# State times queries by four heads at a time: quadrants of the array, two output banks, permuted rows of the first weight matrix

## The chip, the core and the metric

The kernel runs on one core of one Trainium2 chip. The metric is the device time of one execution in microseconds; three executions of the kernel before took 618.56, 619.71 and 620.05 us, median 619.71 us.

## The reference

Three layers follow each other. The first is attention with decay ("retention"): 2 batches, 8 heads, 768 tokens, 64 features a head, in float32. In blocks of tokens

```python
intra = np.einsum('bhic,bhjc->bhij', qb, kb) * Dmask[None]
intra = np.einsum('bhij,bhjd->bhid', intra, vb)
inter = np.einsum('bhid,bhde->bhie', qb * lam_pow[None], kv_state)
out[:, :, sl] = intra + inter
...
kv_state = lam_block[None, :, None, None] * kv_state + np.einsum('bhsd,bhse->bhde', kb_dec, vb)
```

The result, 1536 tokens by 512 features (8 heads of 64), goes through two feed-forward layers: `g(x @ w_in) @ w_out` with `w_in` 512 by 2048 and g a clipped square, then `((x @ w_a) * (x @ w_b)) @ w_out` with inner width 1536. Those weights are float64 in memory.

## The kernel before

**Attention.** It takes blocks of 128 tokens: 12 chunks c, six to a batch. For each chunk `load_chunk` (L143) brings four tiles of 256 KB: q and k by feature (for head h = 2 pr + e, its 64 features stand in partitions 64e to 64e + 63 and its 128 tokens in columns 128 pr), k and v by token. Then, per chunk:

- `att_scores` (L150): eight products of keys and queries, even heads into one PSUM bank, odd heads into another. `att_mask` (L180, VectorE) multiplies both banks with the decay mask into two SBUF tiles.
- `att_kd` (L161) and `att_qd` (L172), on GpSimd: keys and queries times powers of the decay.
- `att_state` (L194, then L205 or L208 and L209): the new state of each head, 64 by 64, kept in `st` with even heads in the lower 64 partitions and odd heads in the upper 64.
- `att_out`: for every chunk but the first of a batch eight products "state times q" (L221), each with 64 rows and 64 columns of TensorE's array; even heads use rows and columns 0 to 63, odd heads rows and columns 64 to 127. Then eight products "weights times v" (L225), with 128 rows and 64 columns, even and odd heads in turn, are added in the same bank. One ScalarE copy (L237) rounds the bank to the type of the matmuls (the "high" part), and one VectorE subtraction (L241) gives the remainder (the "low" part); both stand in `block`, from where `xy` takes them as four groups of 128 features.

Each of these fp32 matmuls is executed as two passes, so the trace has 16 MATMUL records for eight products. PSUM banks come from seven that are handed out in turn (`bank`, L61).

**Feed-forward.** `mm3` (L358) makes each product of three matmuls, high times high, high times low, low times high. `h_bank` is one 128 by 512 tile of the first layer's inner matrix: 12 matmuls, then L376 (VectorE), L377 (ScalarE), L379 (VectorE) and the split of the result by L265 (ScalarE) and L266 (GpSimd). The weights arrive as float64 by `load_w` (L261, issued by SyncE) and are made into high and low tiles by `weight_pieces` (L280 and L281 on ScalarE, L294, L298, L302 and L311 on VectorE, then L265 and L266); `bg(n)` places n such pieces between other work.

**Order.** The order on every engine is written out by hand: chunks 0 to 3 first, then a loop over nb and j in which `h_bank(j, nb)` stands ahead of the output of chunk 4 + 4 nb + j; all of attention is over by 96 us. From then on the feed-forward layers run to the end. SyncE issues the loads in program order; a DMA also waits until the one issued eight places earlier in the program has landed, since all DMAs share eight completion counters in turn.

Of the kernel before, what the change touches and what calls it, by code (L numbers as in the profile page):

```python
# [9 lines left out]
F32 = mybir.dt.float32  # L10
F32R = mybir.dt.float32r
BF16 = mybir.dt.bfloat16
I32 = mybir.dt.int32
U32 = mybir.dt.uint32
ACTF = mybir.ActivationFunctionType
ALU = mybir.AluOpType

B, H, S, D = 2, 8, 768, 64
CH = 128
# [4 lines left out]
KT = DM // 128  # L24
# [11 lines left out]
def retention_ffn_kernel(ctx: ExitStack, tc: tile.TileContext, lam, att, w1i, w1o, w2ab, w2o, out):  # L36
# [7 lines left out]
    nc = tc.nc  # L44
# [9 lines left out]
    block = [const.tile([128, KT, 2, 512], F32R, name=f"block{i}") for i in range(NB)]  # L54
# [6 lines left out]
    def bank():  # L61
        banks.rotate(-1)
        return banks[-1]
# [6 lines left out]
    def free2(*tiles):  # L70
        two.extend(tiles)
# [61 lines left out]
    ck = {}  # L133
    sc = {}
    pm = {}
    kd = {}
    qd = {}
# [73 lines left out]
    def att_out(c):  # L211

        cc = c % CPB
        o = bank()
        s = st[cc % 3]
        pairs = [(pr, slice(pr * 128, (pr + 1) * 128)) for pr in range(H // 2)]
        if cc:
            for pr, cols in pairs:
                for e in range(2):
                    r = slice(64 * e, 64 * e + 64)  # L220
                    nc.tensor.matmul(out=o[r, cols], lhsT=s[r, pr, :], rhs=qd[c][r, cols], start=(pr == 0), stop=False)  # L221
        for pr, cols in pairs:
            for e in range(2):
                h = 2 * pr + e
                nc.tensor.matmul(  # L225
                    out=o[64 * e:64 * e + 64, cols],
                    lhsT=ck[c][3][:, h * D:(h + 1) * D],
                    rhs=pm[c][e][:, pr * CH:(pr + 1) * CH],
                    start=(cc == 0 and pr == 0),
                    stop=(pr == H // 2 - 1),  # L230
                )
        nb, t0 = c // 4, (c % 4) * CH
        if nb not in xy:
            xy[nb] = [block[nb][:, k] for k in range(KT)]
        o4 = o.rearrange("p (a i) -> p a i", a=KT)
        hi, lo = (block[nb][:, :, i, t0:t0 + CH] for i in range(2))
        nc.scalar.copy(hi, o4)  # L237
        free2(*pm.pop(c))
        if cc:
            free2(qd.pop(c))  # L240
        return lambda: nc.vector.tensor_tensor(out=lo, in0=o4, in1=hi.bitcast(F32), op=ALU.subtract)  # L241

    def att_done(c):
        loads.append(ck.pop(c)[3])
# [10 lines left out]
    srcs = {"1i": w1i, "1o": w1o, "2i": w2ab, "2o": w2o}  # L255

    def load_w():
        if todo_loads:
            key = todo_loads.popleft()
            r = raw_p.tile([128, 1024], I32, tag="raw", name="raw")  # L260
            nc.sync.dma_start(out=r, in_=srcs[key[0]][key[1]].bitcast(I32))  # L261
            raws[key] = r

    def split_act(src, hi, lo, engine=None):
# [19 lines left out]
    def weight_pieces():  # L284

        nxt = None
        for n, key in enumerate(order):
# [15 lines left out]
                out=v, in0=high, scalar=-0x40000000, in1=word, op0=ALU.bitwise_and, op1=ALU.bitwise_or  # L303
            )
            load_w()
            if 4 <= n + 1 < len(order):
                if order[n + 1] not in raws:
                    load_w()
                nxt = begin(order[n + 1])
# [210 lines left out]
    powers()  # L520
    load_chunk(0, (0, 1))
    load_w()
    load_chunk(0, (2, 3))
    load_chunk(1, (0, 1))
# [17 lines left out]
    bg(2)  # L542
    att_mask(0)
    low0 = att_out(0)
    att_qd(0, nc.gpsimd)
    att_kd(1, nc.gpsimd)
# [4 lines left out]
    add1 = att_state(1)  # L551
    add1()
    low1 = att_out(1)
    att_done(1)
    att_scores(2)
# [4 lines left out]
    add2 = att_state(2)  # L560
    add2()
    low2 = att_out(2)
    att_done(2)
    bg(1)
# [22 lines left out]
    for nb in range(2):  # L587
        for j in range(4):
            c = 4 + 4 * nb + j
            low = []  # L590
# [6 lines left out]
            low = att_out(c)  # L597
# [33 lines left out]
    for i in range(2, len(stages)):  # L631
        g, nb = stages[i]
# [76 lines left out]
```

## Time and profile before

| | us |
|---|---|
| median of three executions | 619.71 (618.56 to 620.05) |
| the profiled execution | 620.09 |
| span of the profiled execution, first to last instruction | 618.3 |
| TensorE matmuls busy | 597.7 (97% of the span) |
| VectorE busy | 457.3 (74%) |
| GpSimd busy | 278.5 (45%) |
| ScalarE busy | 267.8 (43%) |

PE is TensorE's matmul side and PEld its weight loads; DVE is VectorE, ACT is ScalarE, POOL is GpSimd, SP is SyncE. Times in the trace count from the span's start. Matmuls overlap in the array, so a record's duration is longer than its share of the engine: two records that follow each other closely may start nearly together. An arrow "<-" behind an idle time names what ended it.

### The profile page before, as it was taken

To read this page: it belongs to the slowest core of one execution; us is meant where nothing else is said; L and a number is where in the kernel's file an instruction comes from. 1 tells how busy PE (TensorE), PEld (TensorE's weight loads), DVE (VectorE), ACT (ScalarE), POOL (GpSimd) and SP (SyncE) were. 2 spreads that over 40 slices of the span, in tenths; PEclk is the share of its full clock that TensorE was granted. 3 is DMA by queue.
4 is the path that set the end of the run, shared out by engine and by line. 5 is a ranking of instruction groups with operands and counts; after the bars stand their busy time and mean duration, and the time that the engine had idled before them with its cause. 6 is when DMAs were issued, how large, how long until landed. Compare 5 with 4: busy or idle time off the path is not lost.

```text
span 618.3 us, 8380 instructions
## 1 busy us (share of the span) xinstructions
PE 597.7 (97%) x3100; PEld 488.4 (79%) x3100; DVE 457.3 (74%) x684; ACT 267.8 (43%) x473; POOL 278.5 (45%) x218
## 2 busy tenths in 40 slices
PE   7797899999999999999999999999999999999997
PEld 3676678888888888888888788888888888888886
DVE  1578861964975786497869997989979979979553
ACT  1245552655642553264545456434424424424110
POOL 3535570443522543352947655553453553543420
PEclk9799899999999999999999999999999999999999
DMA  5965520221310212131101222302302202300004
GB/s 176 378 247 203 184 92 1 75 96 68 103 64 10 98 68 69 34 103 49 55 1 35 68 87 83 103 34 90 95 21 96 92 18 93 100 14 1 0 23 182
DMA packets 20937, 52.72 MB, mean 85 GB/s; under 512 B 2584, under 2 KB 4896, under 8 KB 20896
## 3 DMA queue, kind: packets, MB, share of 16 engines
q1 hardware_dynamic: 19624, 51.52, 24.3%
q10 hardware_dynamic: 1272, 0.67, 0.4%
q8 instruction: 24, 0.39, 0.3%
q14 instruction: 17, 0.14, 0.1%
HBM read 49.03 MB, written 3.15 MB: 84 GB/s over the span
## 4 chain that ended last, share of the span: by engine, by line
PE 82%; DVE 8%; ACT 4%; POOL 2%; issue 2%; DMA 1%; ACTq 0%; DVEq 0%; POOLq 0%
PE ps L358 79%; DVE words L294 1%; PE ps L225 1%; PE ps L221 1%; DVE two L302 1%; DVE words L298 1%; DVE two L401 1%; DMA lamp<-in_lam 1%; ACT words L280 1%; DVE two L311 1%; PE ps L150 1%; DVE two L180 1%; DMA rows<-base 1%; ACT four L265 1%; ACT two L281 0%
## 5 line engine op out<-in xcount | busy, mean ns | idle before, releaser
L266 POOL TENSOR_TENSOR four<-two,four 128x512 fp32r<-128x512 f32 x109 | 143.1, 1319 | 213.6 <-ACT four L265 203.4
L358 PE MATMUL ps<-block,four 128*128 128x512 f32 x828 | 196.9, 391 | 1.4 <-POOL block L266 1.4
L358 PEld LDWEIGHTS ps<-block,four 128*128 128x128 f32 x828 | 154.6, 188 | 35.4 <-POOL block L266 1.8
L358 PE MATMUL ps<-four,four 128*128 128x512 f32 x633 | 162.0, 389 | 0.0
L358 PEld LDWEIGHTS ps<-four,four 128*128 128x128 f32 x633 | 118.7, 188 | 24.9 <-issue 0.2
L265 ACT CAST four<-two 128x512 fp32r<-128x512 f32 x109 | 67.1, 620 | 93.4 <-DVE two L451 23.7
L266 POOL TENSOR_TENSOR late_four<-two,late_four 128x512 fp32r<-128x512 f32 x47 | 62.2, 1329 | 56.8 <-ACT late_four L265 49.5
L358 PE MATMUL ps<-block,late_four 128*128 128x512 f32 x324 | 77.2, 389 | 0.0
L358 PEld LDWEIGHTS ps<-block,late_four 128*128 128x128 f32 x324 | 60.8, 188 | 12.6
L280 ACT ACTIVATE words<-raw 128x512 f32<-128x512 f32 x68 | 43.1, 634 | 55.0 <-DVE two L302 49.7
L358 PE MATMUL ps<-four,late_four 128*128 128x512 f32 x243 | 64.0, 389 | 0.0
L377 ACT ACTIVATE two<-two,half 128x512 f32<-128x512 f32 x42 | 30.2, 720 | 70.4 <-DVE two L376 70.4
L294 DVE TENSOR_SCALAR words<-words 128x512 f32<-128x512 f32 x68 | 47.0, 691 | 17.4 <-ACT words L280 17.4
L358 PE MATMUL ps<-late_four,four 128*128 128x512 f32 x213 | 58.5, 389 | 0.0
L358 PEld LDWEIGHTS ps<-four,late_four 128*128 128x128 f32 x243 | 45.6, 188 | 9.5
L464 DVE TENSOR_TENSOR two<-two,ps 128x512 f32<-128x512 f32 x62 | 42.2, 680 | 13.1 <-PE ps L358 13.1
L311 DVE CUSTOM_DVE_ANT_0 two<-two,two 128x1024 uint16<-128x1024 uint16 x54 | 49.7, 921 | 1.9
L376 DVE TENSOR_SCALAR two<-ps 128x512 f32<-128x512 f32 x42 | 28.7, 684 | 29.9 <-PE ps L358 29.4
L298 DVE TENSOR_SCALAR words<-words 128x512 int32<-128x512 int32 x68 | 47.5, 699 | 2.3
L426 DVE TENSOR_TENSOR two<-two,ps 128x512 f32<-128x512 f32 x50 | 32.9, 682 | 19.2 <-PE ps L358 16.7
L358 PEld LDWEIGHTS ps<-late_four,four 128*128 128x128 f32 x213 | 40.0, 188 | 8.3
L265 ACT CAST late_four<-two 128x512 fp32r<-128x512 f32 x47 | 28.9, 620 | 36.4 <-DVE two L440 11.4
(99 smaller groups left out, 596.3 us busy)
## 6 DMA issues: line engine op xcount, KB each, us to landing
load<-in_att SPq DMA_DIRECT2D x48, 256.0 KB, 5.3
raw<-in_w2ab SPq DMA_DIRECT2D x24, 512.0 KB, 3.2
raw<-in_w1i SPq DMA_DIRECT2D x16, 512.0 KB, 3.4
raw<-in_w1o SPq DMA_DIRECT2D x16, 512.0 KB, 3.3
raw<-in_w2o SPq DMA_DIRECT2D x12, 512.0 KB, 3.2
out<-two SPq DMA_DIRECT2D x7, 256.0 KB, 2.0
dmask<-rows SPq DMA_DIRECT2D x2, 256.0 KB, 4.6
out<-late_two SPq DMA_DIRECT2D x2, 256.0 KB, 2.0
```

The source lines that it names most:

```text
L150: nc.tensor.matmul(out=sc[c][h % 2][:, pr * CH:(pr + 1) * CH], lhsT=kT[p0:p0 + 64, pr * CH:(pr + 1) * CH], rhs=qT[p0:p0 + 64, pr * CH:(pr ...
L265: nc.scalar.copy(hi, src)
L266: (engine or nc.gpsimd).tensor_tensor(out=lo, in0=src, in1=hi.bitcast(F32), op=ALU.subtract)
L280: nc.scalar.activation(out=words, in_=r[:, :, 1].bitcast(F32), func=ACTF.Abs)
L294: nc.vector.tensor_scalar(out=words, in0=words, scalar1=HIGH_MIN, scalar2=HIGH_MAX, op0=ALU.max, op1=ALU.min)
L298: nc.vector.tensor_scalar(out=word, in0=word, scalar1=3, scalar2=0x3FFFFFFF, op0=ALU.logical_shift_left, op1=ALU.bitwise_and)
L311: nc.vector.tensor_tensor(out=v, in0=v, in1=c, op=ALU.add)
L358: nc.tensor.matmul(out=ps, lhsT=l[a], rhs=r[b], start=(start and i == 0 and j == 0), stop=(stop and i == n - 1 and j == 2))
L376: nc.vector.tensor_scalar(out=r, in0=ps, scalar1=-1.0, scalar2=1.0, op0=ALU.max, op1=ALU.min)
L377: nc.scalar.activation(out=r, in_=r, func=ACTF.Square, scale=0.5, bias=half)
L426: add = lambda o, x, ps: nc.vector.tensor_tensor(out=o, in0=x, in1=ps, op=ALU.add)
L464: nc.vector.tensor_tensor(out=total, in0=total, in1=ps, op=ALU.add)
```

## The change

`att_out` takes two banks in place of one, one for even heads and one for odd heads. "State times q" goes in two groups of four heads; within a group the four products lie in the four quadrants of the array: even heads in the lower 64 rows and odd heads in the upper 64, as the state lies, and now one even and one odd head in each half of the columns. The eight products of weights and v come even heads first, then odd heads, alternating between the halves of the columns. Each bank is filled in 256 columns, and has its own copy and its own subtraction. The features so come out in another order, and `load_w` brings the rows of the first weight matrix ("1i", 16 tiles) in that order, with four DMAs of 128 KB in place of one of 512 KB, in runs of 1 KB in place of 4 KB.

```diff
     def att_out(c):
-        o = bank()
+        o = [bank(), bank()]
...
         if cc:
-            for pr, cols in pairs:
-                for e in range(2):
-                    r = slice(64 * e, 64 * e + 64)
-                    nc.tensor.matmul(out=o[r, cols], lhsT=s[r, pr, :], rhs=qd[c][r, cols], start=(pr == 0), stop=False)
+            for b in range(2):
+                for e, side in ((0, 0), (1, 1), (0, 1), (1, 0)):
+                    p, w = 64 * e, 2 * b + side
+                    nc.tensor.matmul(
+                        out=o[e][64 * side:64 * side + 64, b * CH:(b + 1) * CH], lhsT=s[p:p + 64, w, :],
+                        rhs=qd[c][p:p + 64, w * CH:(w + 1) * CH], start=(b == 0), stop=False,
+                    )
...
+        for e in range(2):
+            for w in range(H // 2):
+                b, side = w // 2, w % 2
+                h = 2 * w + e
+                nc.tensor.matmul(
+                    out=o[e][64 * side:64 * side + 64, b * CH:(b + 1) * CH],
+                    lhsT=ck[c][3][:, h * D:(h + 1) * D],
+                    rhs=pm[c][e][:, w * CH:(w + 1) * CH],
+                    start=(cc == 0 and b == 0),
+                    stop=(b == 1),
+                )
+            o2 = o[e][:, 0:2 * CH].rearrange("p (a i) -> p a i", a=2)
+            hi, lo = (block[nb][:, 2 * e:2 * e + 2, i, t0:t0 + CH] for i in range(2))
+            nc.scalar.copy(hi, o2)
+            parts.append((lo, o2, hi))
...
+        def low():
+            for lo, o2, hi in parts:
+                nc.vector.tensor_tensor(out=lo, in0=o2, in1=hi.bitcast(F32), op=ALU.subtract)
...
     def load_w():
...
+            if key[0] == "1i":
+                for i in range(4):
+                    side, e = i // 2, i % 2
+                    nc.sync.dma_start(
+                        out=r[64 * side:64 * side + 64, 512 * e:512 * e + 512].rearrange("p (b f) -> p b f", b=2),
+                        in_=src[64 * e:64 * e + 64].rearrange("p (b c f) -> p b c f", b=2, c=2)[:, :, side],
+                    )
```

On TensorE, the output of chunk 1 before (L221 state times q, L225 weights times v; `ps` are banks, `st` the state, `two` the decayed queries or the masked weights, `load` is v):

```order
L221 MATMUL ps_114<-two_99,st_148 64x128 x8
L225 MATMUL ps_114<-two_100,load_126 64x128
L225 MATMUL ps_114<-two_101,load_126 64x128
L225 MATMUL ps_114<-two_100,load_126 64x128
L225 MATMUL ps_114<-two_101,load_126 64x128
...
L150 MATMUL ps_115<-load_127,load_128 128x128
```

and in the changed kernel (L222 and L234 are the new lines of the two products):

```order
L222 MATMUL ps_115<-two_99,st_148 64x128
L222 MATMUL ps_116<-two_99,st_148 64x128
L222 MATMUL ps_115<-two_99,st_148 64x128
L222 MATMUL ps_116<-two_99,st_148 64x128
...
L234 MATMUL ps_115<-two_100,load_126 64x128 x4
L234 MATMUL ps_116<-two_101,load_126 64x128 x4
L150 MATMUL ps_117<-load_127,load_128 128x128
```

The two masked weight tiles, two_100 of the even heads and two_101 of the odd heads, alternated; now the four products that read two_100 stand ahead of the four that read two_101, and the two halves go to two banks. The banks that follow move on by one.

On ScalarE, the copies of chunks 1 and 2 before, then in the changed kernel (L243 is the new line of the copy):

```order
L237 CAST block_71<-ps_114 128x4x128
L208 ACTIVATE st_147<-st_149,tabq 128x64 x4
L237 CAST block_71<-ps_111 128x4x128
L280 ACTIVATE words<-raw 128x512
```

```order
L243 CAST block_71<-ps_115 128x2x128
L243 CAST block_71<-ps_116 128x2x128
L208 ACTIVATE st_147<-st_149,tabq 128x64 x4
L243 CAST block_71<-ps_113 128x2x128
L243 CAST block_71<-ps_114 128x2x128
L302 ACTIVATE words<-raw 128x512
```

One copy of 512 columns became two of 256, in the same place; VectorE's subtractions are split in the same way. L280 and L302 are the same instruction of `weight_pieces` (in the changed file 22 lines lower).

On SyncE, the loads of weight tiles 1i-1 to 1i-3 with chunk 3 between them (load_131 to load_134) and the first of chunk 4 (load_121), before, with the counter that each waits for:

```order
L261 DMA raw<-in_w1i 128x1024 [waits DMAHW5_49]
L143 DMA load_131<-in_att 128x512 [waits DMAHW6_49]
...
L143 DMA load_134<-in_att 128x512 [waits DMAHW1_49]
L261 DMA raw<-in_w1i 128x1024 [waits DMAHW2_49]
L261 DMA raw<-in_w1i 128x1024 [waits DMAHW3_49]
L261 DMA raw<-in_w1o 128x1024 [waits DMAHW4_49,DVE_49,Activation_49]
L143 DMA load_121<-in_att 128x512 [waits DMAHW5_49,Pool_49]
```

and in the changed kernel:

```order
L278 DMA raw<-in_w1i 64x2x256 [waits DMAHW0_49]
...
L143 DMA load_134<-in_att 128x512 [waits DMAHW7_49]
L278 DMA raw<-in_w1i 64x2x256 [waits DMAHW0_49]
L278 DMA raw<-in_w1i 64x2x256 [waits DMAHW1_49]
...
L278 DMA raw<-in_w1i 64x2x256 [waits DMAHW7_49]
L283 DMA raw<-in_w1o 128x1024 [waits DMAHW0_49,DVE_49,Activation_49]
L143 DMA load_121<-in_att 128x512 [waits DMAHW1_49,Pool_49]
```

The quarters of 1i-2 and 1i-3 alone now take all eight counters, and load_121, two places behind them, waits for a quarter of 1i-2 to land.

## Rows read from the trace of the kernel before

**Rows 1.** The page's first part: busy time, share of the span, instructions.

```profile
PE 597.7 (97%) x3100; PEld 488.4 (79%) x3100; DVE 457.3 (74%) x684; ACT 267.8 (43%) x473; POOL 278.5 (45%) x218
```

**Rows 2.** Busy time by stretch, eight stretches from 95 to 618 us: their sum.

```profile
sum 523.00, PE 518.22 PEld 427.94 DVE 399.35 ACT 227.33 POOL 232.26; mean PE 64.78 PEld 53.49 DVE 49.92 ACT 28.42 POOL 29.03
```

**Rows 3.** Chain that ended last, in order of time, 0 to 170 us: start, us, what.

```profile
21.85 1.97 PE ps L221 x16
...
27.96 1.02 PE ps L221 x16
...
30.08 0.59 ACT block L237
...
34.50 1.09 PE ps L225 x14
...
61.31 0.67 DVE block L241
...
68.36 0.57 ACT block L237
...
79.63 1.68 POOL two L172
...
95.51 74.58 PE ps L358 x328
```

**Rows 4.** Timeline of TensorE, three short stretches: start, us, line, count, [idle before].

```profile
18.21 0.32 PE L225 MATMUL ps<-two,load 128*64 128x128 f32 x1 [2.50 <-DVE two L180]
...
87.90 0.33 PE L221 MATMUL ps<-two,st 64*64 64x128 f32 x2
...
88.71 0.28 PE L221 MATMUL ps<-two,st 64*64 64x128 f32 x2
88.92 0.33 PE L225 MATMUL ps<-two,load 128*64 128x128 f32 x2
```

**Rows 5.** Groups by line: names, shapes, count, busy us, mean ns, idle before.

```profile
L241 DVE TENSOR_TENSOR block<-ps,block 128x512 fp32r<-128x512 f32 x12 | 8.3, 690 | 9.4 <-ACT block L237 9.4
...
L237 ACT CAST block<-ps 128x512 fp32r<-128x512 f32 x12 | 7.0, 582 | 12.5 <-PE ps L225 12.5
...
L209 DVE TENSOR_TENSOR st<-st,ps 128x256 f32<-128x256 f32 x8 | 3.3, 418 | 2.0 <-ACT st L208 1.3 <-PE ps L194 0.6
...
L205 ACT COPY st<-ps 128x256 f32<-128x256 f32 x2 | 0.7, 362 | 0.0
```

**Rows 6.** Timeline 56 to 97 us: state times q of chunks 7 and 9.

```profile
64.77 1.97 PE L221 MATMUL ps<-two,st 64*64 64x128 f32 x16 [4.62 <-POOL two L172]
...
81.35 1.09 PE L221 MATMUL ps<-two,st 64*64 64x128 f32 x16 [0.90 <-POOL two L172]
```

**Rows 7.** Busy time by stretch; behind POOL's count stands the granted clock.

```profile
16.57:19.98 3.41, 1.52 (x16) 1.04 (x16) 3.24 (x6) 0.67 (x2) 1.70 (x2) 1.00 1.05 370
19.98:23.39 3.41, 2.67 (x30) 2.48 (x32) 1.11 (x2) 1.50 (x5) 3.41 (x4) 0.50 1.04 391
23.39:26.80 3.41, 3.41 (x31) 2.75 (x30) 0.41 (x1) 1.03 (x4) 2.38 (x3) 0.50 1.05 401
...
64.35:67.76 3.41, 2.99 (x26) 2.66 (x28) 3.38 (x5) 2.27 (x4) 1.64 (x2) 0.50 0.73 219
```

**Rows 8.** Timeline 36 to 60 us: the subtraction of chunk 5 (with the wait before it).

```profile
53.93 0.69 DVE L241 TENSOR_TENSOR block<-ps,block 128x512 fp32r<-128x512 f32 x1 [0.21 <-ACT block L237]
```

**Rows 9.** Line L261, SyncE's issue of the w1i tiles: ns min/median/max, first and last.

```profile
L261 SPq DMA_DIRECT2D raw<-in_w1i x16: 327/328/433, 2.5 to 221.5; - x16
```

**Rows 10.** DMA queues from 18 to 33 us.

```profile
DMA packets 2658, 5.91 MB, mean 394 GB/s; under 512 B 297, under 2 KB 297, under 8 KB 2656
```

**Rows 11.** The page's DMA issues: count, KB each, median us from issue to landing.

```profile
raw<-in_w1i SPq DMA_DIRECT2D x16, 512.0 KB, 3.4
...
dmask<-rows SPq DMA_DIRECT2D x2, 256.0 KB, 4.6
```

**Rows 12.** Timeline 27 to 36 us: chunk 4's decayed keys, chunk 4's scores.

```profile
32.52 1.04 POOL L161 TENSOR_TENSOR two<-load,kdf 128x512 f32<-128x512 f32 x1 [5.21 <-DMA load<-in_att]
...
35.52 0.64 PEld L150 LDWEIGHTS ps<-load,load 64*128 64x128 f32 x10 [0.17 <-issue]
```

More of the change, by code (lines that the diff above doesn't have):

```diff
@@ L213, in att_out @@
         cc = c % CPB
-        o = bank()
+        o = [bank(), bank()]
         s = st[cc % 3]
-        pairs = [(pr, slice(pr * 128, (pr + 1) * 128)) for pr in range(H // 2)]
         if cc:
-            for pr, cols in pairs:
-                for e in range(2):
-                    r = slice(64 * e, 64 * e + 64)
-                    nc.tensor.matmul(out=o[r, cols], lhsT=s[r, pr, :], rhs=qd[c][r, cols], start=(pr == 0), stop=False)
[L222 to L231, printed above, removed]
+            for b in range(2):
[5 more added lines that the diff above has]
+                    )
         nb, t0 = c // 4, (c % 4) * CH
@@ L234, in att_out @@
             xy[nb] = [block[nb][:, k] for k in range(KT)]
-        o4 = o.rearrange("p (a i) -> p a i", a=KT)
-        hi, lo = (block[nb][:, :, i, t0:t0 + CH] for i in range(2))
-        nc.scalar.copy(hi, o4)
+        parts = []
+        for e in range(2):
[13 more added lines that the diff above has]
+            parts.append((lo, o2, hi))
         free2(*pm.pop(c))
@@ L240, in att_out @@
             free2(qd.pop(c))
-        return lambda: nc.vector.tensor_tensor(out=lo, in0=o4, in1=hi.bitcast(F32), op=ALU.subtract)
+        def low():
+            for lo, o2, hi in parts:
+                nc.vector.tensor_tensor(out=lo, in0=o2, in1=hi.bitcast(F32), op=ALU.subtract)
+        return low
     def att_done(c):
@@ L260, in load_w @@
             r = raw_p.tile([128, 1024], I32, tag="raw", name="raw")
-            nc.sync.dma_start(out=r, in_=srcs[key[0]][key[1]].bitcast(I32))
+            src = srcs[key[0]][key[1]].bitcast(I32)
+            if key[0] == "1i":
[5 more added lines that the diff above has]
+                    )
+            else:
+                nc.sync.dma_start(out=r, in_=src)
             raws[key] = r
```

## The prediction

> **What bounds the kernel.** I read the busy times first: TensorE's matmuls fill 97% of the span [rows 1]. Then the stretches: from 95 us to the end TensorE is busy 518.22 of 523.00 us [rows 2], and in the chain of waits one unbroken run of L358 begins at 95.51 [rows 3]. So the feed-forward part is TensorE's, the change doesn't touch its instructions, and what the change can move is when TensorE gets to 95.5 us. Before that the chain changes hands. From 21.85 to 30.08 it is TensorE, with the outputs of chunks 1 and 2. Then it goes to ScalarE's copy at 30.08 and, by way of the masks, to the weights product of chunk 3 at 34.50. From there to 79.63 it is mostly VectorE and ScalarE, and at the end GpSimd with the decayed queries of chunk 9 (L172). From 81.35 it is TensorE again, with the outputs of chunks 9, 10 and 11 [rows 3, 6]. Faster products of state and q count only in the first and the last of these pieces, five of ten chunks; in the middle the same change makes VectorE and ScalarE slower.
>
> **Four quadrants.** The 16 passes of L221 take 1.02 us at the full clock [rows 3]. The timeline shows how: the first two records start together at 87.90, the last two together at 88.71, and the next line follows at 88.92 [rows 4]. So eight pairs follow each other, some 0.11 us apart (0.81 us over seven steps, 0.116). A pair is one even and one odd head, not the two passes of one head: where the odd head still waits for its mask, at 18.21, one record starts alone [rows 4], although that head's second pass is next in the program. The array therefore starts a later head in a free quadrant past the waiting second pass of an earlier one. With four free quadrants I expect four to start together and four rounds in place of eight: 4 x 0.11 = 0.44 us less, 0.58 in place of 1.02. No row shows four at once, so the bounds are 0 and 0.44; I take 0.44, since the pairs already pass over one waiting matmul and each quadrant has only two passes in a group.
> The Trainium skill says otherwise ("TensorE: Matmul & The Clock Gate", section "The mechanism"): matmuls begin and end strictly in program order. By that rule a head's second pass holds up all that follow, no more than two quadrants ever overlap, and the saving would be 0. The record that starts alone, against the two that start together, speaks against it as far as one waiting pass goes [rows 4].
>
> **The sum, along the chain** (lead = how much earlier than before).
> - Chunk 1, at 21.85: the product takes 1.97 us, at a granted clock of 0.50, which is 1.2 GHz and lasts from 19.98 to 26.80 [rows 3, 7]. It saves 0.9. But the clock rises about when it did before, and scores that ran at 2.4 GHz slide into the slow stretch, so half of it is left: 0.45. Chunk 2 at 27.96: 0.44; its masks wait for scores that are earlier too. Say 0.85 together at the end of chunk 2's output.
> - The copy: 582 ns for 512 columns [rows 5]. For 256 the nearest row is the state's copy, 362 ns [rows 5]. The first half's copy runs beside the odd heads' products, so after the last product ScalarE needs 0.36 in place of 0.58: lead 0.85 + 0.22 = 1.07 at 30.08.
> - The subtraction: 690 ns; a half costs what L209 does, 418 [rows 5]. Two make 0.84, 0.15 more. VectorE is behind the copy there, so the masks of chunk 3 keep 0.92.
> - Chunk 3's weights: before, 14 of 16 passes wait for the second mask, because even and odd heads alternate, and take 1.02 us from 34.50 [rows 3] to the scores at 35.52 [rows 12]. Now the eight even passes run during the second mask and eight are left: three rounds fewer, 0.33. Lead 1.25 as the first `h_bank` begins.
> - The middle. Two copies cost 0.72 in place of 0.58: 0.14 each where ScalarE ends last, for chunks 4 and 7 (68.36) [rows 3]. Two subtractions cost 0.15 where VectorE does, chunk 6 (61.31) [rows 3]. For chunk 5 VectorE waits 0.21 for the copy [rows 8]; the first half comes 0.22 sooner, and it evens out. Together 0.43: lead 0.82 as the decayed queries of chunk 9 are ready.
> - Chunks 9, 10, 11 on TensorE: 3 x 0.44 = 1.32.
> Sum: 2.1 us.
>
> **What I cost at nothing.** The banks: chunks of the loop now take six of the seven in an iteration and took five, so scores wait for the product or mask of the iteration before. VectorE has done those before TensorE comes there; by the order of the program the closest is chunk 5's, where the state's addition still ends later. If VectorE fell further behind, scores would wait first. The loads: 16 tiles with three issues more each of 0.33 us [rows 9]; SyncE waits for counters and buffers most of the time. Runs of 1 KB: the mask's table, in runs of 512 B, lands in 4.6 us for 256 KB [rows 11], no worse than the others in that stretch. From 18 to 33 us the queues move 394 GB/s [rows 10] whatever the issue, as long as enough is in flight; that is the third rival.
>
> 620.09 - 2.1 = 618.0 for the profiled execution, which is 0.38 above the median of the three; so 617.6.
>
> **Rivals.**
> - *No more than two quadrants at a time.* Then 0.22 - 0.15 + 0.33 - 0.43: nothing is left, 619.7, the same. For it: no row shows four. Against it: rows 4. The rule of the Trainium skill quoted above would give this time. 0.2.
> - *TensorE, now faster, loses its clock.* Ahead of chunk 9 it waits 0.90 us for GpSimd [rows 6]. The outputs of chunks 7 and 8 lie in front; they become 0.9 (chunk 7 starts at 64.77, at the low clock) and 0.44 shorter, GpSimd is only 0.82 earlier, so the wait grows to 1.3 to 1.9 us. A stretch with little work, 16.57 to 19.98, was followed by one at half the clock that lasted 6.8 us; another lasted 3.4 us [rows 7]. From 81 us on TensorE is the path, so 3.4 us at 1.2 GHz cost 1.7 and 6.8 cost 3.4: 619.3, or with the longer one 620.9, slower than before. The longer one decides the sign. 0.15 in all, a third of it the longer.
> - *The loads come late.* Eight counters filled by quarters hold 1 MB: at 394 GB/s 2.6 us of work. A whole tile lands 3.4 us after its issue [rows 11], 1.3 of it transfer, so a quarter needs about 2.4. That is barely enough; two such rounds (1i-2 and 1i-3, then what waits for them) could cost up to 5 us at worst. Chunk 4's keys land at 32.52, its scores start at 35.52 [rows 12] and would start at 34.3; so from 1.8 us of delay it eats the lead, and 5 us would give 3.2 - 2.1 = 1.1 slower, 620.7. 0.07.
> - Something I didn't price: 0.03.
>
> **How the numbers follow.** A measurement of this kernel can tell about 0.3% (1.9 us) from no change. The forecast, 0.55, is 617.6; its own range is 616.8 (masks or copies overlap better) to 618.6 (a product saves 0.3). It lies just beyond 617.85, so I give it 0.34 of "faster", the rest of it to "same". Unpriced gains add 0.05: faster 0.39. Slower by over 0.3%, above 621.6, needs the long low clock or late loads and more: 0.08. Same 0.53. Range 616.7 to 620.4: it takes in the first rival and most of the second.
>
> **What would show it.** Right: L222 with 16 records in about 0.58 us from its start to the next line, four starting together; L243 near 360 ns and L251 near 420; the first `h_bank` product about 1.2 us earlier, the state products of chunk 9 about 0.8, the long run of L358 about 2.1. Wrong: L222 still near 1.02; a granted clock of 0.50 after 81 us; a wait for DMA ahead of chunk 4's scores; scores waiting for VectorE because of a bank.

## The result and the profile after

The changed kernel takes **622.37 us** (median of 9 runs, 621.56 to 624.51) against 619.47 (617.88 to 621.14, 9 runs) for the kernel before: ratio 1.0051, 95% interval 1.0035 to 1.0068. It is slower by 0.35 to 0.68%, where 617.6 was forecast. The profiled execution took 624.23 us, span 622.4. It is one of the longest of its nine, 1.9 over the median, which matters below where the clock is costed.

The page of the changed kernel, its first part, its DMA total and its chain by engine:

```profile
PE 596.2 (96%) x3100; PEld 487.2 (78%) x3100; DVE 458.0 (74%) x696; ACT 268.5 (43%) x485; POOL 278.3 (45%) x218
...
DMA packets 27849, 52.72 MB, mean 85 GB/s; under 512 B 3352, under 2 KB 13856, under 8 KB 27808
...
PE 80%; DVE 7%; DMA 5%; ACT 3%; SPq 2%; issue 2%; POOL 1%; ACTq 0%; DVEq 0%; POOLq 0%
```

DMA and SyncE's queue now hold 7% of the chain, some 44 us; before, DMA had 1% and SyncE none. To see where the end moved, follow TensorE's timeline (start, us, line, count, idle time before and its releaser). The first stretch is where attention hands over to the feed-forward part, the second chunk 9, the last the long run to the end:

```profile
33.09 1.26 PE L234 MATMUL ps<-two,load 128*64 128x128 f32 x16 [1.43 <-DVE two L180]
37.61 2.08 PE L150 MATMUL ps<-load,load 64*128 64x128 f32 x16 [3.27 <-DMA load<-in_att]
39.62 5.04 PE L380 MATMUL ps<-block,four 128*128 128x512 f32 x12
44.59 1.16 PE L150 MATMUL ps<-load,load 64*128 64x128 f32 x16
...
86.44 0.67 PE L222 MATMUL ps<-two,st 64*64 64x128 f32 x16 [1.04 <-POOL two L172]
...
99.21 11.18 PE L380 MATMUL ps<-four,four 128*128 128x512 f32 x48
```

The scores of chunk 5 (44.59 above) and the long run, in the same view of the kernel before:

```profile
39.71 1.16 PE L150 MATMUL ps<-load,load 64*128 64x128 f32 x16
...
95.44 11.18 PE L358 MATMUL ps<-four,four 128*128 128x512 f32 x48
```

Read it in three steps. Chunk 4's scores (37.61) wait 3.27 us for queries and keys; before, they began at 35.52 with no such wait [rows 12]. The scores and the first `h_bank` products then take 2.08 and 5.04 us, where at the full clock they take 1.16 and 3.0, so that chunk 5's scores come 4.9 us later than before. And the products of state and q of chunk 9 begin at 86.44 (before 81.35 [rows 6]), the long run at 99.21 (before 95.44). So nearly the whole loss is made by 44 us and the tail gives 1.3 of it back. From the long run to the end little changed: 622.4 - 99.2 = 523.2 us, 618.3 - 95.4 = 522.9 before.

The clock, by stretches of that timeline (busy time of the engines, granted clock, DMA share, GB/s):

```profile
33.00:37.16 4.16, 1.26 (x16) 0.83 (x16) 2.82 (x7) 1.36 (x3) 0.00 (x0) 1.00 0.83 282
37.16:43.99 6.83, 6.38 (x26) 5.28 (x27) 1.29 (x2) 0.00 (x0) 3.52 (x3) 0.50 1.00 378
```

TensorE works 1.26 of 4.16 us, and the stretch behind it runs at 0.50 (1.2 GHz), 6.83 us of it. Before, the low stretches of [rows 7] end at 26.80 and begin again at 64.35, with 1.00 between.

Why the keys are late stands in SyncE's queue (issues, in order of time):

```profile
22.83 7.24 SPq L278 DMA_DIRECT2D raw<-in_w1i  x8
30.17 0.52 SPq L283 DMA_DIRECT2D raw<-in_w1o  x1
30.80 5.97 SPq L143 DMA_DIRECT2D load<-in_att  x8
```

The quarters of two tiles hold the queue for 7.24 us, so the loads of chunks 4 and 5 are issued from 30.80 (before from 23.02). And the queues move less while that lasts; 18 to 33 us of the changed kernel, against 394 GB/s before [rows 10]:

```profile
DMA packets 3029, 4.20 MB, mean 280 GB/s; under 512 B 336, under 2 KB 1872, under 8 KB 3027
```

### The profile page after: what moved, and what is told of

Same layout as the page of the kernel before. It is cut to its first block, busy times and chain, and to the rows that moved or that the text cites. A ratio compares the mean times of both kernels' runs of the same rounds, so it can differ in the third digit from the quotient of the medians.

```text
span 622.4 us, 8496 instructions
## 1 busy us (share of the span) xinstructions
PE 596.2 (96%) x3100; PEld 487.2 (78%) x3100; DVE 458.0 (74%) x696; ACT 268.5 (43%) x485; POOL 278.3 (45%) x218
## 4 chain that ended last, share of the span: by engine, by line
PE 80%; DVE 7%; DMA 5%; ACT 3%; SPq 2%; issue 2%; POOL 1%; ACTq 0%; DVEq 0%; POOLq 0%
PE ps L380 78%; DMA load<-in_att 2%; DMA raw<-in_w1i 1%; SPq L143 1%; DMA tabq<-rows 1%; DVE two L423 1%; DVE words L316 1%; DVE words L320 1%; SPq L278 1%; DVE two L324 1%; DMA rows<-base 1%; DVE two L333 1%; DVE two L180 1%; ACT words L302 1%; PE ps L234 0%
## 5 line engine op out<-in xcount | busy, mean ns | idle before, releaser
L380 PE MATMUL ps<-block,four 128*128 128x512 f32 x828 | 199.0, 394 | 2.1 <-POOL block L288 1.4
L380 PEld LDWEIGHTS ps<-block,four 128*128 128x128 f32 x828 | 156.0, 190 | 36.7 <-POOL block L288 1.8
L380 PE MATMUL ps<-four,four 128*128 128x512 f32 x633 | 162.0, 389 | 0.0
L380 PEld LDWEIGHTS ps<-four,four 128*128 128x128 f32 x633 | 118.7, 188 | 24.9 <-issue 0.2
L380 PE MATMUL ps<-block,late_four 128*128 128x512 f32 x324 | 77.2, 389 | 0.0
L380 PEld LDWEIGHTS ps<-block,late_four 128*128 128x128 f32 x324 | 60.8, 188 | 12.6
L302 ACT ACTIVATE words<-raw 128x512 f32<-128x512 f32 x68 | 43.1, 634 | 55.4 <-DVE two L324 50.1
L380 PE MATMUL ps<-four,late_four 128*128 128x512 f32 x243 | 64.0, 389 | 0.0
L380 PE MATMUL ps<-late_four,four 128*128 128x512 f32 x213 | 58.5, 389 | 0.0
L380 PEld LDWEIGHTS ps<-four,late_four 128*128 128x128 f32 x243 | 45.6, 188 | 9.5
L380 PEld LDWEIGHTS ps<-late_four,four 128*128 128x128 f32 x213 | 40.0, 188 | 8.3
```

The costliest lines, as they stand in the source:

```text
L302: nc.scalar.activation(out=words, in_=r[:, :, 1].bitcast(F32), func=ACTF.Abs)
L380: nc.tensor.matmul(out=ps, lhsT=l[a], rhs=r[b], start=(start and i == 0 and j == 0), stop=(stop and i == n - 1 and j == 2))
```

## The experiments

**Theory:** the quarter loads of the first weight matrix (`w1i`) cost it, by a wait ahead of chunk 4 and a low clock behind it, and the attention part gained what was forecast. **Rivals:** the second bank or the copies in halves cost it; the clock alone; and, within the loads, their number, their short runs, or something else. Each comparison is with the kernel before on the same chip; "long run" is where L380 or its equivalent begins in the profile.

**1. The order of rows made on the host, whole loads** (`e1_host_order`).

```diff
-            if key[0] == "1i":
...
+            nc.sync.dma_start(out=r, in_=src)
...
-        "w1i": tiles(inputs["moe_w_in"]),
+        "w1i": tiles(inputs["moe_w_in"]).reshape(-1, 2, 64, 2, 2, 128).transpose(0, 4, 2, 1, 3, 5).reshape(-1, 128, 512),
```

> The change with its attention untouched, but the rows of the first weight matrix are put in the new order when the inputs are laid out, so that each tile is one load of 512 KB again. Theory (the loads in quarters cost some 7 us, by way of the wait ahead of chunk 4's scores and of the low clock behind it; quadrants and banks gain what the prediction's sum said): 617.5 us, 0.3% below the kernel before; no wait for DMA ahead of chunk 4's scores, they start near 34.5 us, the long run of the feed-forward products near 93.5. Rival (the second bank, or the copies and subtractions in halves, cost it): near 622, and the wait moves to VectorE or ScalarE.

Measured: 616.91 us, ratio 0.9959 (0.9941 to 0.9976), long run at 92.3. TensorE's timeline, and the queues from 18 to 33 us:

```profile
33.73 1.16 PE L150 MATMUL ps<-load,load 64*128 64x128 f32 x16
34.83 3.06 PE L371 MATMUL ps<-block,four 128*128 128x512 f32 x12
...
79.54 0.67 PE L222 MATMUL ps<-two,st 64*64 64x128 f32 x16 [1.64 <-POOL two L172]
```

```profile
DMA packets 2660, 5.92 MB, mean 395 GB/s; under 512 B 296, under 2 KB 296, under 8 KB 2658
```

No wait, full clock, 0.4% faster than before. The rest of the change is a gain of 2.5 us, the loads a loss of 5.5 (622.37 - 616.91). As causes of the loss, banks and halves are out.

**2. The kernel before, with the loads in quarters** (`e2_before_quarters`).

```diff
+                for i in range(4):
+                    side, e = i // 2, i % 2
+                    nc.sync.dma_start(
+                        out=r[64 * side:64 * side + 64].rearrange("p (b c f) -> p b c f", b=2, c=2)[:, :, e],
+                        in_=src[64 * side:64 * side + 64].rearrange("p (b c f) -> p b c f", b=2, c=2)[:, :, e],
+                    )
```

> The kernel before, its attention untouched; only each tile of the first weight matrix is loaded in four quarters of 64 rows with two runs of 1 KB, each to the place it had. Theory (loads): chunk 4's keys land 5 us later, its scores start near 37.6 in place of 35.5, and a stretch at half the clock behind them costs 2 to 3 more: 624, 0.7% slower than before. Rival (banks or halves): 619.5, as before, with the loads' wait hidden.

Measured: 622.51 us, 1.0048 (1.0029 to 1.0067), long run at 97.5. The same two marks on TensorE's timeline:

```profile
35.93 1.95 PE L150 MATMUL ps<-load,load 64*128 64x128 f32 x16 [2.19 <-DMA load<-in_att]
37.81 3.82 PE L367 MATMUL ps<-block,four 128*128 128x512 f32 x12
```

The quarters alone, put into the kernel before, bring the wait, the low clock and 3.1 us (622.51 against 619.40 on that chip), less than the 5.5 of experiment 1 and than the 624 expected. The keys come earlier than in the changed kernel (the scores begin at 35.93, not 37.61), and in this profile TensorE ran at the full clock from 23 to 28 us, where before it had 0.62, so that much of the delay was made up ahead of chunk 4: its scores begin only 0.4 us later than before, and chunk 5's, behind the low clock, 1.9 later (41.56 against 39.71).

**3 and 4. Number or short runs?** Four loads of 32 whole rows each (`e4_four_rows`), and one load in 512 runs of 1 KB (`e5_one_dma_1k`), both on experiment 1.

```diff
+                for i in range(4):
+                    nc.sync.dma_start(out=r[32 * i:32 * i + 32], in_=src[32 * i:32 * i + 32])
```

```diff
+                nc.sync.dma_start(out=r.rearrange("p (b f) -> p b f", b=4), in_=src.rearrange("b p f -> p b f"))
...
+        "w1i": tiles(inputs["moe_w_in"]).reshape(-1, 2, 64, 2, 2, 128).transpose(0, 1, 3, 4, 2, 5).reshape(-1, 4, 128, 128),
```

> As e1_host_order, but each tile in four loads of 32 whole rows (runs of 4 KB in place of 1 KB). Theory by the number of loads (each takes one of eight completion counters and an issue of SyncE's): chunk 4 waits as in the change, 622. Theory by the runs (1 KB runs move fewer bytes per second, and make an issue take 0.6 us in place of 0.33): 617.5, as e1_host_order, and an issue of 0.33 us.

> As e1_host_order, but each tile is one load of 512 KB in 512 runs of 1 KB (the four column blocks of a tile lie apart in memory). Theory by the number of loads: 617.5, as e1_host_order. Theory by the runs: chunk 4 waits as in the change, 621 to 622, and one issue takes 1 us or more.

Measured: 621.65 us, 1.0043 (1.0028 to 1.0059), and 617.45, 0.9967 (0.9954 to 0.9980). The queues from 18 to 33 us in the one with four loads of whole rows, then in the one with short runs:

```profile
DMA packets 1799, 4.07 MB, mean 272 GB/s; under 512 B 328, under 2 KB 328, under 8 KB 1797
```

```profile
DMA packets 3675, 5.67 MB, mean 378 GB/s; under 512 B 281, under 2 KB 1817, under 8 KB 3673
```

Runs of 1 KB cost 4% of the rate and 0.5 us in the medians (617.45 against 616.91, in spreads that overlap); the loss is there without them. I took that for the number of loads. It was only half an answer.

**5. Halves by rows** (`e11_halves`), on experiment 1.

```diff
+                for i in range(2):
+                    nc.sync.dma_start(out=r[64 * i:64 * i + 64], in_=src[64 * i:64 * i + 64])
```

> As e1_host_order (616.9), but each tile of the first weight matrix in two loads of 64 whole rows, 256 KB each as the loads of the chunks. Theory by the counters (a load waits for the one eight before it, so that what is in flight is at most eight loads; eight of 256 KB kept the queues full before): 616.9 to 617.3, chunk 4 doesn't wait. Theory by a cost of each load on the queues: a third of what four loads a tile cost (621.65 - 616.91), 618.5, and fewer GB/s from 18 to 33 us.

Measured: 621.59 us, 1.0036 (1.0020 to 1.0052). Neither expectation holds: two loads a tile lose as much as four. The stretches show a third thing (columns as above; the last two are DMA share and GB/s), here and then in experiment 1:

```profile
23.00:28.00 5.00, 5.00 (x80) 4.15 (x80) 2.13 (x5) 1.71 (x6) 2.08 (x2) 0.72 1.06 307
28.00:33.00 5.00, 3.64 (x76) 2.80 (x64) 3.38 (x8) 2.84 (x8) 2.27 (x2) 1.00 1.02 252
```

```profile
23.00:28.00 5.00, 5.00 (x72) 4.31 (x70) 2.23 (x5) 1.71 (x6) 3.35 (x3) 0.69 1.04 401
28.00:33.00 5.00, 3.58 (x72) 2.94 (x68) 3.39 (x7) 2.84 (x8) 0.17 (x1) 1.00 1.05 390
```

The DMA engines are busy all the time (1.06, 1.02) and move 252 to 307 GB/s; in experiment 1, as busy, they moved 390 to 401. So the DMA engines don't lack work there. The load itself is slow.

**6 and 7. The same cut by columns** (`e13_halves_by_column`, `e14_quarters_by_column`): each load writes all 128 rows. The edit of the halves; the quarters have four loads of 256 columns.

```diff
+                for i in range(2):
+                    cols = slice(512 * i, 512 * i + 512)
+                    nc.sync.dma_start(out=r[:, cols], in_=src[:, cols])
```

> As e11_halves (two loads of 256 KB a tile, 621.6), but cut by columns: each load writes all 128 rows, 2 KB of each, in place of 64 rows of 4 KB. Theory by the rows that a load covers (a load into 64 rows moves at about half the rate of one into 128, which would be why e11_halves is slow although eight of its loads are in flight): 617.0, 390 GB/s from 23 to 33 us, no wait ahead of chunk 4. Theory by the number of loads alone: 621.6, as e11_halves.

> As e4_four_rows (four loads of 128 KB a tile, 621.65), but cut by columns: each load writes all 128 rows, 1 KB of each. The issues and the places among the eight counters are the change's, the rows a load covers are not. Theory by the rows alone: 617. Theory by the number (e12_tiny_loads shows that three more loads a tile are late even when they carry nothing): 620 to 622, and under 350 GB/s from 23 to 33 us. Both at work: between, 618 to 620.

Measured: halves 616.97, 0.9959 (0.9945 to 0.9973); quarters 618.00, 0.9987 (0.9968 to 1.0007). The two stretches, halves and then quarters:

```profile
23.00:28.00 5.00, 5.00 (x68) 4.28 (x64) 1.95 (x4) 1.70 (x6) 2.20 (x3) 0.63 1.06 390
28.00:33.00 5.00, 3.58 (x72) 2.97 (x70) 3.39 (x8) 2.82 (x8) 1.14 (x1) 1.00 1.06 392
```

```profile
23.00:28.00 5.00, 5.00 (x88) 4.30 (x86) 2.46 (x5) 2.60 (x9) 2.56 (x3) 0.94 0.86 294
28.00:33.00 5.00, 2.98 (x58) 2.13 (x54) 4.54 (x10) 2.67 (x8) 0.31 (x1) 1.00 0.82 298
```

With the same number of loads and the same bytes in each, halves of 128 rows cost nothing and halves of 64 rows 4.6 us. That is the cause: **a load into 64 (or 32) of the 128 rows is slow**. It isn't the pieces: the changed kernel and experiment 7 both bring 128 KB in 128 runs of 1 KB, and with 64 rows take 622.37 us, with 128 rows 618.00. Nor is it when the loads behind them are issued: halves by rows let chunk 4's loads go from 26.72 us, quarters by column only from 27.52, yet chunk 4's scores begin at 36.70 in the one and at 34.21 in the other.

The number comes second. Quarters by column leave the DMA engines idle in part (DMA share 0.86, 0.82) and cost 1.0 us in the median, in a wide spread from 616.92 to 622.45: the profiled execution, of 620.90, waits 1.80 us ahead of chunk 4; that the shorter ones don't is read from their times alone. The changed kernel shows both, first the low rate at full share, then gaps:

```profile
23.00:28.00 5.00, 5.00 (x68) 4.25 (x64) 1.70 (x4) 1.70 (x6) 1.30 (x2) 0.61 1.08 306
28.00:33.00 5.00, 3.65 (x76) 2.88 (x68) 3.38 (x8) 2.83 (x8) 2.27 (x2) 1.00 0.77 207
```

The Trainium skill has the first effect ("SBUF — State Buffer", section "Door 1: The DMA port swizzle (why `[64,N]` ≈ `[32,N]`)"): transfers pass through 16 ports, and rows 0 to 63 (partitions) reach only 8 of them, no more than rows 0 to 31 do. Its two measured rates, for transfers of 1 MiB, are 196 GB/s for 64 rows and 328 for 128. The trace agrees in direction, with 252 against 392 GB/s between 28 and 33 us (other, whole loads are mixed in here); and experiments 3 and 5, with 32 and 64 rows, lose the same. That the ports are the reason no run here shows.

**8. The number alone** (`e12_tiny_loads`).

```diff
+    spare = const.tile([1, 48], F32, name="spare")
...
+                for i in range(3):
+                    n = 3 * key[1] + i
+                    nc.sync.dma_start(out=spare[0:1, n:n + 1], in_=lam[0:1])
```

> As e1_host_order, each tile whole again, but behind each of the 16 loads three loads of one number (4 bytes of the decay rates into a spare tile that nothing reads), so that the number of loads is the change's and the bytes and runs are those of e1_host_order. Theory by the counters and issues (tiny loads take places among eight as quarters do, and what waits behind them is late): chunk 4 waits again, 620 to 622, and fewer than 350 GB/s from 18 to 33 us. Theory by a cost of splitting the bytes (a quarter moves slower while it moves): 616.9 to 617.5 and 390 GB/s.

Measured: 624.01 us, 1.0079 (1.0062 to 1.0096). This median is no measure of the loads. The long run begins at 94.22, 1.9 us later than in experiment 1, but then lasts 527.8 us, where it lasts 522.8 to 523.3 in all other profiles. TensorE is never idle in the stretch from 150 to 200 us, at a clock of 1.00, and does 220 products there where experiment 1 does 222:

```profile
150.00:200.00 50.00, 50.00 (x220) 41.10 (x219) 34.12 (x51) 20.89 (x35) 17.37 (x14) 1.00 0.16 53
```

Those 5 us are unexplained (the spare tile also moves what is allocated after it in memory; not tried). What it does show is the first part: chunk 4 waits 2.12 us for its keys although the extra loads carry 4 bytes each, and the queues move 327 GB/s from 18 to 33 us, with a DMA share of 0.76 from 28 to 33. It agrees with experiment 7: places in the queue count, too.

**9. The clock apart from the wait** (`e6_idle`).

```diff
     low3()
+    warm(16)
+    banks.rotate(1)
     att_scores(4)
```

> The change as it is, with 16 idle products (128x512, of zeros, into the bank that chunk 4's scores take next) ahead of chunk 4's scores, where TensorE waits 3.27 us for keys and queries. They leave nothing out. Theory (TensorE's idle time there costs twice, the wait itself and then a stretch at half the clock): the wait stays, scores of chunk 4 near 37.8, but at a granted clock of 1.00 they take 1.1 and the first feed-forward product 3.0 us; 2.5 to 3 us of the change's time come back, 619.5. Rival (the low clock there has nothing to do with the wait): the stretch at half the clock stays and the time is 622.4 or a little more.

Measured: 621.60 us, 1.0034 (1.0021 to 1.0047), long run at 96.1. TensorE's timeline:

```profile
34.18 3.40 PE L115 MATMUL ps<-idle 128*128 128x512 bf16 x15 [0.16 <-issue]
37.52 1.16 PE L150 MATMUL ps<-load,load 64*128 64x128 f32 x16
38.61 3.02 PE L380 MATMUL ps<-block,four 128*128 128x512 f32 x12
```

The wait stays, and the clock stays up: 1.16 and 3.02 us in place of 2.08 and 5.04. So it is TensorE's idle time that lets the clock fall. In the two profiles this brings 3.2 us (99.2 to 96.1), but in the medians only 0.8, and the intervals overlap. The profile of the changed kernel is one of its longest. Against experiment 1 its chunk 4 scores begin 3.9 us later (37.6 against 33.7), and scores and first products lose 2.9 to the clock; in experiment 3 it is 2.2 (35.9) and 1.6 (1.16 + 4.61 against 1.16 + 3.0), and in experiment 2 the clock takes 1.6, too. So how the 5.5 us of the medians divide is not shown: the wait is the larger part in both profiles, and idle products, which take the low clock away, bring back 0.8, not clear of noise. How often the longer drop occurs was not counted.

**10. The last of the four tiles behind chunk 4's loads** (`e9_later_loads`). The first tile of `w1o`, which follows it in the queue, moves with it.

```diff
     load_chunk(3)
-    load_w()
-    load_w()
     warm(8)
...
     load_chunk(4)
+    load_w()
+    load_w()
     att_scores(3)
```

> The change as it is, quarters and all, but the last tile of the first four of the first weight matrix is loaded behind chunk 4's loads in place of ahead of them. Theory (the quarters cost time only because chunk 4's keys and queries stand behind eight of them in the queue): keys and queries land 3 us earlier, no wait for DMA and no low clock ahead of the feed-forward part, 618, if the later tile isn't missed. Rival (the number of loads costs bandwidth wherever they stand): 621 to 622.5.

Measured: 619.36 us, 0.9999 (0.9981 to 1.0017). Timeline of TensorE:

```profile
31.45 0.69 PE L194 MATMUL ps<-load,two 128*64 128x64 f32 x16 [1.34 <-POOL two L161]
...
35.65 1.35 PE L150 MATMUL ps<-load,load 64*128 64x128 f32 x16
36.92 3.01 PE L380 MATMUL ps<-block,four 128*128 128x512 f32 x12
40.99 1.16 PE L150 MATMUL ps<-load,load 64*128 64x128 f32 x16 [1.06 <-DMA load<-in_att]
```

Chunk 4 no longer waits for DMA, and 3.0 of the 5.5 us are back, but not all (618 was expected): chunk 3's state product waits 1.34 us for GpSimd's decayed keys (in experiment 1 it begins at 29.85), a low clock follows (0.66 from 32 to 37 us), and chunk 5's scores wait for DMA in their turn. The shortage is moved along the queue, not removed.

**11. Two quadrants at a time** (`e7_pairs`), on experiment 1.

```diff
-            for b in range(2):
-                for e, side in ((0, 0), (1, 1), (0, 1), (1, 0)):
+            for first in range(2):
+                for b, e, side in ((0, 0, first), (0, 1, 1 - first), (1, 0, first), (1, 1, 1 - first)):
```

> As e1_host_order (616.9), but the products of state and q in an order in which four of a kind use only two quadrants and the next four only the other two. Theory (a free quadrant takes a later product, past those that wait, and four quadrants save 0.44 us a chunk against two): a product of 16 passes takes 0.9 to 1.0 us again and 5 chunks of them cost 2 us: 619. Rival (strict order, or any order does, since the array looks far ahead): 0.60 us and 616.9.

Measured: 616.97 us, 0.9962 (0.9948 to 0.9976), as experiment 1: my expectation was wrong and the rival's number right. TensorE's timeline, the first records of one chunk's products, and the last with the line that follows:

```profile
85.78 0.35 PE L222 MATMUL ps<-two,st 64*64 64x128 f32 x4
...
86.16 0.30 PE L222 MATMUL ps<-two,st 64*64 64x128 f32 x4
86.39 0.33 PE L234 MATMUL ps<-two,load 128*64 128x128 f32 x2
```

Four start together at 85.78, and the next line follows 0.61 us after them. The first four products in the program use two quadrants, and two quadrants never start more than two records together [rows 4]. So two of the four belong to the fifth and sixth products, past two whole products that wait. The order among the quadrants doesn't matter; that all four are used does. The Trainium skill's strict order, which the prediction set against this ("TensorE: Matmul & The Clock Gate", section "The mechanism"), would have given pairs here; the run goes against it.

**12. The next wait** (`e10_queries_first`): experiment 1 leaves TensorE waiting 1.64 us for the decayed queries of chunk 9.

```diff
-                att_kd(c + 1, nc.gpsimd)
                 att_qd(c + 1, nc.gpsimd)
+                att_kd(c + 1, nc.gpsimd)
```

> As e1_host_order, but in the loop over chunks GpSimd makes the decayed queries ahead of the decayed keys, since outputs want the queries first. In e1_host_order TensorE waits 1.64 us for the queries of chunk 9 at 79.54. Theory (that wait is the next bound of the path): up to 1.0 us less, 616.0, and a wait of 0.6 there. Rival (the keys become the wait, at the product for the state, or the weights of 1o come later behind them): 616.9, the wait moves to L194.

Measured: **615.84 us**, 0.9938 (0.9918 to 0.9958), the fastest of all. Its timeline at chunk 9, and the long run:

```profile
78.39 0.67 PE L222 MATMUL ps<-two,st 64*64 64x128 f32 x16 [0.27 <-POOL two L172]
...
91.19 11.18 PE L371 MATMUL ps<-four,four 128*128 128x512 f32 x48
```

The wait falls from 1.64 to 0.27 (0.6 was expected), and no wait for the keys takes its place. The gain is 1.1 us, where up to 1.0 was expected.

## Why the prediction was wrong

**The step that failed** is "What I cost at nothing. … The loads: 16 tiles with three issues more each of 0.33 us [rows 9]; SyncE waits for counters and buffers most of the time", and the sentence behind it, "From 18 to 33 us the queues move 394 GB/s [rows 10] whatever the issue, as long as enough is in flight". This term of nothing measured 5.5 us (experiment 1). Three things went wrong there. An issue of a quarter takes 0.60 us, not 0.33; what that costs by itself is not shown. This is the changed kernel's line (ns min/median/max):

```profile
L278 SPq DMA_DIRECT2D raw<-in_w1i x64: 533/601/1294, 2.5 to 227.1; - x64
```

Next, 394 GB/s is the rate of loads into all 128 rows; of the loads of before only the two of the decay table write 64 rows, and I didn't look at them. I asked about the length of the runs (1 KB, 0.5 us in the medians, experiment 4) and not about the rows that a load covers, which cost 4.6 us (experiments 5 and 6). Last, the third rival did say where it would strike, a wait for DMA ahead of chunk 4's scores, and priced the delay of the keys at up to 5 us; they came 5.7 us late (the decayed keys of chunk 4 begin at 38.19, not 32.52 [rows 12]). But that was taken for the worst case and given 0.07, with no price for the low clock behind it. The rival took 3.2 us for the loss, where the medians have 5.5: of what is missing, 0.7 is the longer delay of the keys, and the low clock took 1.6 to 2.9 us in the profiles; the exact split stays open. (Its 620.7 should be 620.8 by its own terms, 619.7 + 1.1.)

**The second rival**, TensorE losing its clock after a wait, was right as a mechanism and wrong in its place: it came at 37 us, behind the wait for DMA, and not ahead of chunk 9, where 1.04 us (1.64 in experiment 1, in the 1.3 to 1.9 forecast) of waiting left the clock at 1.00.

**Steps that held**, in the changed kernel: L222 in 0.60 us in place of 1.02 (97.59 to 98.19), four starting together, close to the 0.44 forecast; L243 and L251 at the sizes forecast. The first records of one chunk's products, then the groups by line (count, busy us, mean ns, idle before):

```profile
97.59 0.34 PE L222 MATMUL ps<-two,st 64*64 64x128 f32 x4
```

```profile
L251 DVE TENSOR_TENSOR block<-ps,block 128x256 fp32r<-128x256 f32 x24 | 9.2, 417 | 4.9 <-ACT block L243 4.9
...
L243 ACT CAST block<-ps 128x256 fp32r<-128x256 f32 x24 | 8.1, 371 | 9.3 <-PE ps L234 8.1 <-DVE two L180 1.2
```

**The sum** can be checked in experiment 1, the change without its loads; its chain in order of time:

```profile
28.87 0.37 ACT block L243
29.24 0.55 ACT words L293
...
66.49 0.64 ACT block L243 x2
...
92.39 223.28 PE ps L371 x984
```

- Chunks 1 and 2: forecast 0.85 earlier, measured 1.21 (copy at 28.87 against 30.08 [rows 3]); chunk 1's part, halved to 0.45 in the step, is 0.78: chunk 2's scores begin at 24.88 and began at 25.66.
- The copy: forecast lead 1.07, measured 1.43 (29.24 against 30.67, the end of the copy in [rows 3]): the 0.22 of the step held.
- Masks and weights of chunk 3: forecast lead 1.25, measured 1.79 (scores at 33.73 against 35.52 [rows 12]).
- The middle: forecast 0.43 lost, measured nothing: chunk 9 at 79.54 against 81.35 [rows 6], still 1.81. Two halves back to back overlap, which accounts for part of it: the two copies at 66.49 take 0.64 on the chain, 0.06 more than the 0.58 of one whole copy [rows 5], not 0.14.
- The tail: forecast 1.32, measured 3.12 - 1.81 = 1.31.

In all 3.1 us in the profiles (618.3 to 615.2) and 2.5 in the medians, where 2.1 was forecast. The 1.0 that the profiles gain beyond the forecast is 0.54 ahead of chunk 4's scores (1.79 for 1.25) and the 0.43 of the middle that did not come.

## What to carry to other kernels

Before you split a load, ask which of the 128 rows each piece writes: halves cut by columns kept the rate (quarters of 128 KB left gaps), pieces cut by rows lost a fifth to a third of it, and a permutation of rows belongs into the layout of the input, where it cost the device nothing. A load that is late ahead of a TensorE stage was paid twice in these profiles, once as the wait and once in the clock behind it, so a rival of that kind has to be priced with both. And a resource that the trace of before shows at one pattern only (here 128 rows, eight loads in flight) is not measured for the pattern that the change brings.

## What the runs showed of the hardware that was not expected

- Stretches with loads into 64 rows keep the DMA engines as busy (1.02 to 1.06) at 252 to 307 GB/s as loads into 128 rows at 390; four loads into 32 rows lose no more time than two into 64 (621.65 and 621.59 us).
- Runs of 1 KB in one load of 512 KB move 378 GB/s against 395 for runs of 4 KB.
- In fp32, products in a free quadrant start past at least two whole products that wait for theirs (experiment 11); 16 passes over four quadrants take 0.60 us, over two 1.02.
- Two copies or subtractions of half the size, back to back, take about 0.06 us more than a whole one, not the 0.14 that their single durations give.
- A wait of 3.27 us of TensorE was followed by 6.83 us at half the clock; filled with idle products, the clock stayed at full, while a wait of 1.64 us ahead of chunk 9 didn't lower it.
